# Linear attention beside a SwiGLU block: the order of x loads, statistics and normalisation around sixteen projection tiles

## The chip, the cores and the metric

The kernel runs on one core of a Trainium2 chip. The metric is the device time of one execution in microseconds (us). Five engines work side by side, each through its own list of instructions in order: TensorE (PE), ScalarE (ACT), VectorE (DVE), GpSimd (POOL) and SyncE (SP). SP and ACT also issue DMAs, each on a queue of its own.

## The reference

The input is x (2048 x 512), with bf16 weights. Both branches read the same layer-normalised rows.

```python
xn = _layernorm(x)                        # mean and variance over 512
q, k, v = split(xn @ wqkv)                # 32 heads of 16
pq, pk = phi(q), phi(k)                   # phi(t) = where(t > 0, t + 1, exp(t)) + 1e-6
kv = einsum("bhsd,bhse->bhde", pk, v);  z = sum over s of pk
o  = (pq @ kv) / (pq . z + 1e-6)
g  = silu(xn @ w_gate);  u = xn @ w_up    # F = 1792
out = x + o @ wo + (g * u) @ w_down
```

## The kernel before

The 2048 rows are cut into 16 tiles of 128 (`NT`). Row p*16 + t of x is partition p of tile t, so one DMA can load several neighbouring tiles for all partitions. The program writes down, tile by tile, what each engine does. `_Prog` turns this into one list per engine, in the order of writing, and adds a semaphore wait wherever an operation reads or overwrites what another engine or a DMA has written. Nothing is reordered afterwards: the order of the text is the order of the work on each engine.

First stage, per tile t:

- `xload` (L197) brings x; `wqkv_load` (L204) brings quarters of the q and k weights (128 rows each).
- DVE computes the statistics: `bns(t)` (bn_stats, L289) and `agg(t)` (bn_aggr, L292). `rstd_pow(t)` then adds epsilon (L310; on DVE for the tiles in `VD`, on POOL for the others) and POOL raises to the power -0.5 (L317). `stat(t)` is the three in a row.
- `xn_dve(t)` (L297) normalises into `xn_sb`. `xn(t)` does that and, from tile 3 on, issues a DMA transpose on SP (`transpose_dma`, L380) into `xnT`, which PE needs as the stationary operand. Tiles 0 to 2 are transposed on PE, by hand-written steps with filler matmuls in between.
- PE computes `kproj(t)` and `qproj(t)` (L389; the first parts at L402), four matmuls each. ACT takes the exponentials (L425, L431) and copies q (L435). `feat_k(t)` on DVE clips (L442) and adds max(k, 0) (L451) to give pk; POOL adds up z from pk (`zsum`, L507), two tiles behind.
- `gtacc(t)` (L515) accumulates xn transposed times pk in four PSUM banks. The product with the v weights is taken only once, after all tiles.

The start is written out by hand to tile 3. From tile 4 a loop runs, and two tables, `STAT` and `XN`, say after the features of which tile a later tile's statistics and normalisation are placed:

```python
STAT = {4: (8,), 5: (9,), 6: (10,), 7: (11, 12), 8: (13,), 9: (14, 15)}
XN = {4: (7,), 5: (8,), 6: (9,), 7: (10,), 8: (11, 12), 9: (13,), 10: (14, 15)}
```

In iteration 10, behind the transposes of tiles 14 and 15, SP issues tile 0's transpose (wanted only by the second stage), then the first halves of the gate and up weights (`whalf`, L219), the v weights, the output weights and the second half of the gate weights.

The second stage is the feed-forward: for each of four chunks of 512 rows and 14 column blocks, PE computes gate and up (L648), ACT the silu (L663) and DVE the product (L669). The attention output's matrices (L746, L769), the normalisation of pq by its denominator (L778 to L811) and the output tiles (L820, L831, L844) are woven in between. The first feed-forward matmuls need `xnT` of tiles 0 to 3 and the first weight halves.

Of the kernel before, what the change touches and what calls it, by code (L numbers as in the profile page):

```python
# [108 lines left out]
def bass_parallel_sum__linear_attn_block__swiglu_ffn__prompt_kernel(  # L109
# [13 lines left out]
    pe, act, dve, pool, sp = nc.tensor, nc.scalar, nc.vector, nc.gpsimd, nc.sync  # L123
    bf, f32 = dt.bfloat16, dt.float32

    with contextlib.ExitStack() as es:
        E = es.enter_context

        def sb(name, shape, d=bf):
            return E(nc.sbuf_tensor(name, [P] + shape, d))  # L130
# [6 lines left out]
        xnT = sb("xnT", [NDC, S])  # L137
# [50 lines left out]
        def bk(i):  # L188
            return ("bank", i)
# [5 lines left out]
        def xload(eng, h, t0, n, after=()):  # L195
            K.dma(
                eng, lambda: h.dma_start(x_sb[:, t0:t0 + n, :], xv[:, t0:t0 + n, :]),  # L197
                r=list(after), w=[("x", t0 + i) for i in range(n)],
            )

        def wqkv_load(eng, h, name, i, c0, n, after=()):
            K.dma(
                eng,
                lambda: h.dma_start(  # L204
                    wqkv_sb[:, c0:c0 + n, i * D:(i + 1) * D],
                    A_wqkv[c0 * P:(c0 + n) * P, i * D:(i + 1) * D].rearrange("(c p) f -> p c f", p=P),
                ),
                r=list(after), w=[(name, c0)],
            )
# [6 lines left out]
        def whalf(name, dst, src, h):  # L216
# [19 lines left out]
            r=[("ident",)], w=[("ident",)],  # L236
# [6 lines left out]
        wqkv_load("sp", sp, "wk", 1, 2, 2)  # L243
        xload("act", act, 2, 1)
        wqkv_load("act", act, "wq", 0, 0, 2)
        wqkv_load("sp", sp, "wq", 0, 2, 2)
        xload("act", act, 3, 1)
        xload("sp", sp, 4, 1)
        xload("act", act, 5, 1)
        xload("sp", sp, 6, 4, [("wq", 0), ("wq", 2)])  # L250
        xload("sp", sp, 10, 2)
        xload("sp", sp, 12, 4)

        cw = nc.const_aps.tensor(1.0, (P, P), bf)
        cx = nc.const_aps.tensor(1.0, (P, 512), bf)
# [32 lines left out]
        def bns(t):  # L288
            K.op("dve", lambda: dve.bn_stats(stats[:, t, :], x_sb[:, t, :]), r=[("x", t)], w=[("st", t)])  # L289

        def agg(t):
            K.op("dve", lambda: dve.bn_aggr(mv[:, t, :], stats[:, t, :]), r=[("st", t)], w=[("mv", t)])  # L292
# [8 lines left out]
                r=[("x", t), ("mv", t), ("rstd", t)], w=[("xn", t)],  # L301
            )

        VD = (1, 2, 3, 4)

        def rstd_pow(t):
            eng, h = ("dve", dve) if t in VD else ("pool", pool)
            K.op(
                eng,
                lambda: h.tensor_scalar(  # L310
                    out=vpe[:, t:t + 1], in0=mv[:, t, 1:2], scalar1=1e-5, scalar2=None, op0=ALU.add,
                ),
                r=[("mv", t)], w=[("vpe", t)],
            )
            K.op(
                "pool",
                lambda: pool.tensor_tensor(out=rstd[:, t:t + 1], in0=vpe[:, t:t + 1], in1=nhalf[:, :], op=ALU.pow),  # L317
                r=[("vpe", t), ("nhalf",)], w=[("rstd", t)],
            )

        def transpose_pe(t, b):
            tb = banks[b].bitcast(bf)[:, 0:512].rearrange("p (c s) -> p c s", c=NDC)
            K.op(
                "pe",
                [
                    (lambda c=c: pe.transpose(tb[:, c, :], xn_sb[:, t, c * P:(c + 1) * P], ident[:, :]))
                    for c in range(NDC)
                ],
                r=[("xn", t), ("ident",)], w=[bk(b)],
            )  # L330
            K.op(
                "act",
                lambda: act.activation(xnT[:, :, t * P:(t + 1) * P], tb, ACT.Copy),
                r=[bk(b)], w=[("xnT", t)],
            )
# [41 lines left out]
        def transpose_dma(t):  # L377
            K.dma(
                "sp",
                lambda: sp.dma_start_transpose(out=xnT[:, :, t * P:(t + 1) * P], in_=xn_sb[:, t, :]),  # L380
                r=[("xn", t)], w=[("xnT", t)],
            )


        def proj(t, b, lo, wname):
            K.op(
                "pe",
                [
                    (lambda c=c: pe.matmul(  # L389
                        banks[b], xnT[:, c, t * P:(t + 1) * P], wqkv_sb[:, c, lo:lo + D],  # L390
                        start=(c == 0), stop=(c == NDC - 1),
                    ))
                    for c in range(NDC)
                ],
                r=[("xnT", t), (wname, 0), (wname, 2)], w=[bk(b)],
            )

        def proj_part(src, key, b, lo, wname, h):
            K.op(
                "pe",  # L400
                [
                    (lambda c=c: pe.matmul(  # L402
                        banks[b], src[:, c, :], wqkv_sb[:, c, lo:lo + D],
                        start=(c == 0), stop=(c == NDC - 1),
                    ))
                    for c in (2 * h, 2 * h + 1)
                ],
                r=[key, (wname, 2 * h)], w=[bk(b)],
            )

        def kb(t):
            return 2 * (t % 2)

        def qb(t):
            return 2 * (t % 2) + 1

        def kproj(t):
            proj(t, kb(t), D, "wk")

        def qproj(t):  # L420
            proj(t, qb(t), 0, "wq")
# [7 lines left out]
        def exp_q(t):  # L429
            K.op(  # L430
                "act", lambda: act.activation(eq[:, t, :], banks[qb(t)], ACT.Exp),  # L431
                r=[bk(qb(t))], w=[("eq", t)],
            )
            K.op(
                "act", lambda: act.activation(pkq[:, t, 1, :], banks[qb(t)], ACT.Copy),  # L435
                r=[bk(qb(t))], w=[("pq", t)],
            )

        def clip(e, res):
            K.op(  # L440
                "dve",
                lambda: dve.tensor_scalar(  # L442
                    out=e, in0=e, scalar1=1.0, scalar2=1e-6, op0=ALU.min, op1=ALU.add,
                ),
                r=[res], w=[res],
            )

        def maxadd(dst, src, e, r, w):
            K.op(
                "dve",  # L450
                lambda: dve.scalar_tensor_tensor(  # L451
                    out=dst, in0=src, scalar=0.0, in1=e, op0=ALU.max, op1=ALU.add,
                ),
                r=r, w=w,
            )
# [25 lines left out]
        def first_feat():  # L481
            K.op(
                "dve",
                lambda: dve.tensor_tensor(out=pkq[:, 0, 0, :], in0=kpos[:, :], in1=ek[:, 0, :], op=ALU.add),
                r=[("kpos",), ("ek", 0)], w=[("pk", 0)],
            )

        def feat_k(t):
            e = t % NE
            clip(ek[:, e, :], ("ek", e))  # L490
            if t >= 2:
                zsum(t - 2, e)
            maxadd(pkq[:, t, 0, :], banks[kb(t)], ek[:, e, :], [bk(kb(t)), ("ek", e)], [("pk", t)])
# [30 lines left out]
        def stat(t):  # L524
            bns(t)
            agg(t)
            rstd_pow(t)

        def xn(t):
            xn_dve(t)  # L530
            if t >= 3:
                transpose_dma(t)

        bns(0)
        agg(0)
# [33 lines left out]
        agg(3)  # L569
        rstd_pow(3)  # L570
        first_feat()
        transpose_pe(2, 4)
        exp_k(1)
        first_eq()
        first_pq()
        qproj(1)
        kproj(2)
        xn(3)
        bns(4)
        agg(4)  # L580
        rstd_pow(4)
        feat_k(1)
        bns(5)
        xn(4)
        agg(5)
        rstd_pow(5)
        exp_q(1)
        exp_k(2)
        gtacc(0)
# [1 line left out]
        exp_q(2)  # L591
        gtacc(1)
        feat_k(2)
        stat(6)
        xn(5)
        kproj(3)
        exp_k(3)
        qproj(3)
        exp_q(3)
        feat_k(3)  # L600
        stat(7)
        xn(6)
        gtacc(2)

        STAT = {4: (8,), 5: (9,), 6: (10,), 7: (11, 12), 8: (13,), 9: (14, 15)}
        XN = {4: (7,), 5: (8,), 6: (9,), 7: (10,), 8: (11, 12), 9: (13,), 10: (14, 15)}

        for t in range(4, NT):
            kproj(t)
            exp_k(t)  # L610
            qproj(t)
            exp_q(t)
            feat_k(t)
            for i in STAT.get(t, ()):
                stat(i)
            for i in XN.get(t, ()):
                xn(i)
            if t == 10:
                transpose_dma(0)
                whalf("wg", wg_sb, B_w_gate, 0)  # L620
                whalf("wu", wu_sb, B_w_up, 0)
                wqkv_load("sp", sp, "wv", 2, 0, 4)
                wload("sp", sp, "wo", wo_sb, A_wo)
                whalf("wg", wg_sb, B_w_gate, 1)
            if t == 12:
                masks()
            if t >= 12:
                gtacc(t - 2)
            elif t < 11:
                gtacc(t - 1)  # L630
# [242 lines left out]
        for j in range(NJ):  # L873
# [11 lines left out]
            if NORM0 <= j < NORM0 + 3 * NT:  # L885
                i, ph = (j - NORM0) // 3, (j - NORM0) % 3
# [41 lines left out]
```

## Time and profile before

| | us |
|---|---|
| median of 3 runs | 214.53 |
| lowest, highest | 214.12, 214.85 |
| profiled execution | 215.17 |
| its span, first to last instruction | 213.9 |
| PE busy | 208.8 (98%) |
| DVE busy | 119.8 (56%) |
| POOL busy | 72.5 (34%) |
| ACT busy | 68.2 (32%) |
| mean granted clock of PE | 1.000 |

The profile shows one execution. Its span runs from the first to the last instruction; the device time includes what lies around it. Busy time counts computing instructions alone, not an engine's waits or the issue of DMAs. Matmuls overlap their neighbours and their ends are modelled, so the busy share of PE is a reading of how closely matmuls follow each other. Idle time of an engine matters only where the chain of waits passes through it. Times within the span are counted from its start: the projection stage lasts to 51.0 us, the second stage from there to the end.

### The profile page before, as it was taken

What the parts mean: (1) busy time and instruction counts of PE and PEld (TensorE: products, weight loads), DVE (VectorE), ACT (ScalarE), POOL (GpSimd) and SP (SyncE); (2) the same over time, 40 slices, a digit from 0 to 9 for tenths busy, and PEclk for the clock granted to TensorE, in tenths of its full rate; (3) what the DMA queues carried; (4) which work ended last, traced back from release to release, by engine and by line L of the source; (5) the groups of instructions that cost most, each with busy time, mean ns of one, the idle gap of its engine ahead of it and who ended that gap; (6) DMA issues with size and microseconds to landing.
All of it is one profiled execution on the core that took longest, in us unless ns stands there. A gap on an engine that the chain in (4) does not pass through costs nothing.

```text
span 213.9 us, 2779 instructions
## 1 busy us (share of the span) xinstructions
PE 208.8 (98%) x1001; PEld 96.7 (45%) x1001; DVE 119.8 (56%) x245; ACT 68.2 (32%) x119; POOL 72.5 (34%) x92
## 2 busy tenths in 40 slices
PE   8979989999999999999999999999999999999996
PEld 3434434444544444444444444444444444444454
DVE  4796888634454777355463765463656436374121
ACT  3476665666453332112031313122132213121000
POOL 3346777758104244042221441221404141222100
PEclk9999999999999999999999999999999999999999
DMA  5682233389994011102101011101011010110101
GB/s 184 242 211 49 49 31 72 77 272 365 225 368 124 0 25 25 49 3 49 25 26 49 0 28 49 29 20 49 3 49 25 25 25 28 27 48 26 49 28 51
DMA packets 28319, 16.45 MB, mean 77 GB/s; under 512 B 19088, under 2 KB 27920, under 8 KB 28304
## 3 DMA queue, kind: packets, MB, share of 16 engines
q1 hardware_dynamic: 27328, 15.34, 27.7%
q10 hardware_dynamic: 976, 0.92, 1.3%
q8 instruction: 8, 0.13, 0.3%
q14 instruction: 7, 0.06, 0.1%
HBM read 9.70 MB, written 2.10 MB: 55 GB/s over the span
## 4 chain that ended last, share of the span: by engine, by line
PE 89%; DMA 4%; DVE 4%; ACT 1%; issue 0%; POOL 0%; ACTq 0%
PE psum L648 45%; PE psum L831 23%; PE psum L389 7%; PE psum L820 6%; DMA xnT<-xn_sb 4%; PE psum L515 4%; PE psum L261 2%; DVE stats L289 1%; DVE pkq L451 1%; ACT ek L425 1%; DVE ek L442 1%; PE psum L402 0%; POOL rstd L317 0%; PE psum L746 0%; PE psum L769 0%
## 5 line engine op out<-in xcount | busy, mean ns | idle before, releaser
L663 ACT ACTIVATE sg<-psum 128x512 bf16<-128x512 f32 x56 | 33.4, 598 | 106.8 <-PE psum L648 106.0
L648 PE MATMUL psum<-xnT,wu_sb 128*128 128x512 bf16 x224 | 57.5, 379 | 0.0
L648 PE MATMUL psum<-xnT,wg_sb 128*128 128x512 bf16 x224 | 57.5, 379 | 0.0
L778 POOL TENSOR_TENSOR prod<-pkq,zb 128x512 f32<-128x512 bf16 x16 | 18.6, 1160 | 57.8 <-DVE pkq L451 57.8
L648 PEld LDWEIGHTS psum<-xnT,wu_sb 128*128 128x128 bf16 x224 | 21.9, 98 | 26.4 <-issue 0.2
L648 PEld LDWEIGHTS psum<-xnT,wg_sb 128*128 128x128 bf16 x224 | 21.9, 98 | 26.2
L844 DVE TENSOR_TENSOR out_sb<-psum,x_sb 128x512 bf16<-128x512 f32 (+1 forms) x17 | 11.2, 660 | 36.1 <-PE psum L831 36.1
L669 DVE TENSOR_TENSOR pkq<-psum,sg 128x512 bf16<-128x512 f32 x28 | 19.2, 687 | 18.6 <-PE psum L648 14.1
L802 POOL TENSOR_TENSOR pqn<-pkq,rden 128x512 bf16<-128x512 bf16 x16 | 16.9, 1055 | 36.6 <-DVE rden L796 36.6
L389 PE MATMUL psum<-wqkv_sb,xnT 128*128 128x512 bf16 x116 | 27.3, 379 | 1.9 <-DMA xnT<-xn_sb 1.9
L669 DVE TENSOR_TENSOR xn_sb<-psum,sg 128x512 bf16<-128x512 f32 x28 | 18.8, 671 | 14.2 <-PE psum L648 13.6
L831 PE MATMUL psum<-wd_sb,xn_sb 128*128 128x512 bf16 (+1 forms) x126 | 25.7, 355 | 0.0
L831 PE MATMUL psum<-wd_sb,pkq 128*128 128x512 bf16 x112 | 25.5, 379 | 0.0
L507 POOL TENSOR_TENSOR zacc<-zacc,pkq 128x512 f32<-128x512 f32 x15 | 17.3, 1155 | 6.4 <-DVE ek L442 6.0
L389 PEld LDWEIGHTS psum<-wqkv_sb,xnT 128*128 128x128 bf16 x116 | 11.1, 98 | 16.0 <-DMA xnT<-xn_sb 1.7
L831 PEld LDWEIGHTS psum<-wd_sb,xn_sb 128*128 128x128 bf16 x126 | 12.3, 98 | 11.9
L831 PEld LDWEIGHTS psum<-wd_sb,pkq 128*128 128x128 bf16 x112 | 11.0, 98 | 13.2
L820 PE MATMUL psum<-m_sb,eq 128*128 128x512 bf16 (+1 forms) x68 | 16.6, 366 | 0.0
L515 PE MATMUL psum<-pkq,xn_sb 128*128 128x512 bf16 x64 | 16.1, 379 | 0.0
L786 DVE TENSOR_REDUCE den<-prod 128x32 f32<-128x512 f32 x16 | 10.9, 684 | 5.7 <-POOL prod L778 5.7
L289 DVE BATCH_NORM_STATS2 stats<-x_sb 128x6 f32<-128x512 bf16 x16 | 10.9, 682 | 3.0 <-DMA x_sb<-in_A_x_dram 3.0
L425 ACT ACTIVATE ek<-psum 128x512 bf16<-128x512 f32 x15 | 9.0, 600 | 10.4 <-DVE mv L292 2.8
(67 smaller groups left out, 135.6 us busy)
## 6 DMA issues: line engine op xcount, KB each, us to landing
out_dram<-out_sb SPq DMA_DIRECT2D x15, 128.0 KB, 1.7
wg_sb<-in_B_w_gate_dram SPq DMA_DIRECT2D x2, 896.0 KB, 8.3
wu_sb<-in_B_w_up_dram SPq DMA_DIRECT2D x2, 896.0 KB, 6.7
wd_sb<-in_B_w_down_dram SPq DMA_DIRECT2D x1, 1792.0 KB, 9.7
x_sb<-in_A_x_dram SPq DMA_DIRECT2D x2, 512.0 KB, 4.4
wqkv_sb<-in_A_wqkv_dram ACTq DMA_DIRECT2D x2, 256.0 KB, 4.1
wqkv_sb<-in_A_wqkv_dram SPq DMA_DIRECT2D x2, 256.0 KB, 5.5
wqkv_sb<-in_A_wqkv_dram SPq DMA_DIRECT2D x1, 512.0 KB, 9.2
```

Of the source, the lines that this page charges most:

```text
L289: K.op("dve", lambda: dve.bn_stats(stats[:, t, :], x_sb[:, t, :]), r=[("x", t)], w=[("st", t)])
L389: (lambda c=c: pe.matmul(banks[b], xnT[:, c, t * P:(t + 1) * P], wqkv_sb[:, c, lo:lo + D], start=(c == 0), stop=(c == NDC - 1),))
L507: lambda: pool.tensor_tensor(out=zacc[:, :], in0=zacc[:, :], in1=pk, op=ALU.add),
L515: (lambda c=c: pe.matmul(banks[4 + c], xn_sb[:, t, c * P:(c + 1) * P], pkq[:, t, 0, :], start=(t == 0), stop=(t == NT - 1),))
L648: (lambda c=c: pe.matmul(banks[b], w_sb[:, c, fc * P:(fc + 1) * P], xnT[:, c, C * 512:(C + 1) * 512], start=(c == 0), stop=(c == NDC - 1),))
L663: lambda: act.activation(sg[:, j % NSG, :], banks[gb], ACT.Silu),
L669: lambda: dve.tensor_tensor(out=hT(C, fc), in0=banks[ub], in1=sg[:, j % NSG, :], op=ALU.mult,),
L778: lambda: pool.tensor_tensor(out=p, in0=pkq[:, t, 1, :], in1=zb[:, :], op=ALU.mult),
L802: lambda: pool.tensor_tensor(out=pqn[:, t % NPN, :].rearrange("p (h e) -> p h e", e=DH), in0=pkq[:, t, 1, :].rearrange("p (h e) -> p h e", ...
L820: (lambda g=g: pe.matmul(dst, pqnT(t)[:, g, :], m_sb[:, g, lo:hi], start=(g == 0), stop=False,))
L831: (lambda fc=fc: pe.matmul(dst, hT(C, fc)[:, jj * P:(jj + 1) * P], wd_sb[:, fc, lo:hi], start=False, stop=(fc == NFC - 1),))
L844: lambda: dve.tensor_tensor(out=o, in0=src, in1=x_sb[:, t, lo:hi], op=ALU.add),
```

## The change

The x loads of tiles 8 to 15 are no longer issued in a row on SP at the start. They go two tiles at a time, each behind one DMA transpose on SP: tiles 8 and 9 behind tile 3's, 10 and 11 behind tile 5's, 12 and 13 behind tile 6's, 14 and 15 behind tile 7's. Of the initial loads, tiles 6 and 7 remain as one.

The second half of the q weights is split into quarters: the third goes on SP's queue, the fourth on ACT's, ahead of x tile 3. Readers of the q weights wait for both, and so does the load of tiles 6 and 7.

Statistics are placed about a tile earlier. In the start, `bns(4)` stands ahead of `xn(3)`. In the loop, `STAT` places tile t+5 behind the features of tile t, and `XN0` places normalisations in front of the features, where `XN` had them behind. `VD` loses tile 4, whose epsilon is then added on POOL. Tile 0's DMA transpose moves from iteration 10 to iteration 7.

```diff
--- before
+++ after
@@ -243,13 +243,12 @@
         wqkv_load("sp", sp, "wk", 1, 2, 2)
         xload("act", act, 2, 1)
         wqkv_load("act", act, "wq", 0, 0, 2)
-        wqkv_load("sp", sp, "wq", 0, 2, 2)
+        wqkv_load("sp", sp, "wq", 0, 2, 1)
+        wqkv_load("act", act, "wq", 0, 3, 1)
         xload("act", act, 3, 1)
         xload("sp", sp, 4, 1)
         xload("act", act, 5, 1)
-        xload("sp", sp, 6, 4, [("wq", 0), ("wq", 2)])
-        xload("sp", sp, 10, 2)
-        xload("sp", sp, 12, 4)
+        xload("sp", sp, 6, 2, [("wq", 0), ("wq", 2), ("wq", 3)])
 
         cw = nc.const_aps.tensor(1.0, (P, P), bf)
         cx = nc.const_aps.tensor(1.0, (P, 512), bf)
@@ -301,7 +300,7 @@
                 r=[("x", t), ("mv", t), ("rstd", t)], w=[("xn", t)],
             )
 
-        VD = (1, 2, 3, 4)
+        VD = (1, 2, 3)
 
         def rstd_pow(t):
             eng, h = ("dve", dve) if t in VD else ("pool", pool)
@@ -392,7 +391,7 @@
                     ))
                     for c in range(NDC)
                 ],
-                r=[("xnT", t), (wname, 0), (wname, 2)], w=[bk(b)],
+                r=[("xnT", t), (wname, 0), (wname, 2)] + ([(wname, 3)] if wname == "wq" else []), w=[bk(b)],
             )
 
         def proj_part(src, key, b, lo, wname, h):
@@ -405,7 +404,7 @@
                     ))
                     for c in (2 * h, 2 * h + 1)
                 ],
-                r=[key, (wname, 2 * h)], w=[bk(b)],
+                r=[key, (wname, 2 * h)] + ([(wname, 3)] if wname == "wq" and h else []), w=[bk(b)],
             )
 
         def kb(t):
@@ -530,6 +529,10 @@
             xn_dve(t)
             if t >= 3:
                 transpose_dma(t)
+            if t == 3:
+                xload("sp", sp, 8, 2)
+            elif 5 <= t < 8:
+                xload("sp", sp, 2 * t, 2)
 
         bns(0)
         agg(0)
@@ -569,21 +572,22 @@
         agg(3)
         rstd_pow(3)
         first_feat()
+        bns(4)
+        xn(3)
+        agg(4)
+        rstd_pow(4)
         transpose_pe(2, 4)
         exp_k(1)
         first_eq()
         first_pq()
         qproj(1)
         kproj(2)
-        xn(3)
-        bns(4)
-        agg(4)
-        rstd_pow(4)
         feat_k(1)
         bns(5)
-        xn(4)
         agg(5)
         rstd_pow(5)
+        xn(4)
+        stat(6)
         exp_q(1)
         exp_k(2)
         gtacc(0)
@@ -591,32 +595,36 @@
         exp_q(2)
         gtacc(1)
         feat_k(2)
-        stat(6)
         xn(5)
+        stat(7)
         kproj(3)
         exp_k(3)
         qproj(3)
         exp_q(3)
+        xn(6)
         feat_k(3)
-        stat(7)
-        xn(6)
+        stat(8)
         gtacc(2)
 
-        STAT = {4: (8,), 5: (9,), 6: (10,), 7: (11, 12), 8: (13,), 9: (14, 15)}
-        XN = {4: (7,), 5: (8,), 6: (9,), 7: (10,), 8: (11, 12), 9: (13,), 10: (14, 15)}
+        STAT = {4: (9,), 5: (10,), 6: (11,), 7: (12, 13), 8: (14,), 9: (15,)}
+        XN0 = {4: (7,), 5: (8,), 6: (9,), 7: (10,), 8: (11,), 9: (12, 13), 10: (14, 15)}
+        XN = {}
 
         for t in range(4, NT):
             kproj(t)
             exp_k(t)
             qproj(t)
             exp_q(t)
+            for i in XN0.get(t, ()):
+                xn(i)
             feat_k(t)
             for i in STAT.get(t, ()):
                 stat(i)
             for i in XN.get(t, ()):
                 xn(i)
+            if t == 7:
+                transpose_dma(0)
             if t == 10:
-                transpose_dma(0)
                 whalf("wg", wg_sb, B_w_gate, 0)
                 whalf("wu", wu_sb, B_w_up, 0)
                 wqkv_load("sp", sp, "wv", 2, 0, 4)
```

## The prediction

> **What bounds the kernel now.** I first read busy time by engine and the chain of work that ended last: TensorE (PE) is busy 208.8 of 213.9 us, at full granted clock in all 40 slices, and carries 89% of the chain. So only a wait on PE's path can be worth time. The waits of PE, longest first, are three besides the start:
>
> ```profile
> PE psum L389 <- DMA xnT<-xn_sb: 1.9, 2, 1.2
> PE psum L261 <- PEq L913: 0.8, 1, 0.8
> PE psum L402 <- DMA wqkv_sb<-in_A_wqkv_dram: 0.3, 1, 0.3
> ```
>
> The timeline of PE places them. Columns are start, time, engine, line, operands; the bracket is the idle time before and what ended it:
>
> ```profile
> 7.50 0.59 PE L402 MATMUL psum<-wqkv_sb,xcT 128*128 128x512 bf16 x2
> 8.37 0.60 PE L402 MATMUL psum<-wqkv_sb,xcT 128*128 128x512 bf16 x2 [0.27 <-DMA wqkv_sb<-in_A_wqkv_dram]
> ...
> 13.35 1.03 PE L515 MATMUL psum<-pkq,xn_sb 128*128 128x512 bf16 x4
> 15.59 1.90 PE L389 MATMUL psum<-wqkv_sb,xnT 128*128 128x512 bf16 x8 [1.22 <-DMA xnT<-xn_sb]
> ...
> 30.28 1.03 PE L515 MATMUL psum<-pkq,xn_sb 128*128 128x512 bf16 x4
> 32.03 1.89 PE L389 MATMUL psum<-wqkv_sb,xnT 128*128 128x512 bf16 x8 [0.73 <-DMA xnT<-xn_sb]
> ```
>
> The bracket undercounts. A group of four that is followed without a wait hands over after 0.86 us (at 11.62, next at 12.49), though its modelled end is 1.03 after its start. PE could have gone on at 13.35 + 0.86 = 14.21 and at 30.28 + 0.86 = 31.14, so the two pauses cost 1.38 and 0.89 us: **2.27 us** on the path. In front of 8.37 the same reading gives 0.43.
>
> Why the data were late stands in the chain of waits and in the DMAs' issues and landings:
>
> ```profile
> 11.00 4.55 DMA xnT<-xn_sb
> 15.54 0.05 issue
> 15.59 1.90 PE psum L389 x8
> ...
> 27.28 4.62 DMA xnT<-xn_sb
> 31.90 0.14 issue
> ```
>
> Both are DMA transposes (L380), of tile 3 and of tile 9. The median of the 14 is 2.4 us from issue to landing; these two took 4.55 and 4.62. In front of tile 3's, on the same SP queue, went the x loads of tiles 6 to 9, 10 to 11 and 12 to 15, issued at 8.40, 8.79 and 9.26; the last landed at 14.90, the transpose 0.64 later. Tile 9's met no load. In its stretch (27 to 32 us) the DMA view shows two instruction fetches:
>
> ```profile
> q14 instruction: 1, 0.01, 1.8%
> q8 instruction: 1, 0.02, 1.8%
> ```
>
> In a usual 2.4 it would have landed at 29.7, 1.4 before PE's need at 31.14. So one transpose waits behind traffic, the other had too little lead.
>
> **The change part by part.**
>
> *x loads behind the transposes.* This takes 768 KB out of the way of tile 3's transpose (only tiles 6 and 7, 256 KB, stay ahead). Its normalisation waits today until 10.56 for rstd (0.44 of idle). In that hole now goes tile 4's bn_stats: the row L289 gives 0.61 us to the next start, so from 10.03 (the first features' start at 9.43, its 0.68 less an overlap of 0.08) to 10.64. The normalisation starts 0.08 later and the transpose at about 11.08. Its landing is bounded by 2.4 (median) and 4.55 (the row with 768 KB ahead). I take 2.5: the first x load, twice this size, landed 3.18 after its issue, at 11.58, while a transpose's own packets come in its second half. It lands at 13.6 against a need at 14.21, and the 1.38 goes. At the bad end, 15.63, 1.42 us remain.
>
> *What is late next.* Tile 4: PE wants it at 14.21 + 2.59 (the spacing of tiles in the PE rows) = 16.80. DVE's order is now clip and max-add of tile 1 (11.22 to 12.2, after ek at 11.18), bn_stats 5, aggregate, normalisation 4, ending near 13.35. The x load of tiles 8 and 9 is issued ahead of its transpose, at 12.4. By the 2.4 row it lands at 15.8, by 4.55 at 17.9. I take 16.1 (behind a 256 KB load that lands near 15.4): no wait. Tiles 5 to 8 follow the same sum and land 1 to 3 us ahead.
>
> *Statistics and normalisation a tile ahead.* In the loop, normalisation of tile t+3 stands before the features of tile t. Tile 9's comes near 23.0, its transpose at 23.3, landing 25.7 against a need at 14.21 + 6 x 2.59 = 29.75. A fetch that adds 2.2 (4.62 less 2.41) is covered, whichever transpose it hits: the 0.89 goes. DVE does the same work: 2.13 us of a tile's 2.59 (19.95 to 22.08), and its cyclic order stays clip, max-add, statistics, normalisation.
>
> *x data for DVE.* bn_stats of tile 8 comes near 17.3, its load is issued at 12.4; with the longest landing of any x load, 6.2, it is there at 18.6. A late one delays normalisation 7 (near 18.1) by 1.3, and its transpose still lands near 22.3, against 24.6. Later pairs have more. SP's queue gains three 0.45 us issues between transposes of 1.2: it stays under the 2.59 per tile.
>
> *VD without tile 4.* The add of epsilon goes from DVE (0.15) to POOL (0.22 to 0.39) ahead of a pow of 0.6; rstd is there at 12.1, the normalisation starts at 12.97: nothing.
>
> *Transpose of tile 0 and the weights.* SP issues the gate and up weights after the last transposes, today at 42.74 and 43.38. The up half lands at 51.64 and its first matmul starts at 51.89: 0.25 us of cover for a path that moves forward by 2.27. In the new order normalisations 14 and 15 stand before the features of tile 10. Normalisation 15 waits for its rstd until 34.45; the transposes issue at 33.7 and 34.9, tile 0's is no longer between, and the weights go out near 36.1. With 8.3 to landing, the up half is there by 45, before its need at 49.6. That hides; without it all but 0.25 us would be given back.
>
> *wq in two quarters, the second on ACT's queue.* The last of wq landed at 8.32, x tile 3 (the last of 768 KB on ACT's queue) at 8.14. Shifting 128 KB, wq should be complete near 8.14 (gain up to 0.18). x tile 3 lands later, by 0.1 to at most 0.81 (by 8.95 all ten loads had landed). It feeds bn_stats 3 at 8.24, then normalisation 2, which ends at 9.24 against PE's transpose at 9.68: 0.4 of cover, so at worst +0.3. Bounds -0.2 to +0.3; I take 0.
> The Trainium skill (DMA: Bandwidth & Descriptors, Queues, rings and completion order) says each DMA engine takes turns between the queues it has work for. That gives the same lateness of x tile 3, and the trace agrees: 896 KB on each queue, last landings 8.95 and 8.78.
>
> **Sum.** Profiled execution: 215.17 us, span 213.9 and 1.27 around it. Less 1.38 and 0.89 it is 212.9. The median of the three runs is 0.64 lower than that execution, 214.53; the same subtraction gives 212.3. All after the projections is PE work back to back and moves as one block.
>
> **Rivals.**
>
> *The SP queue still stretches the transposes.* Loads are now woven between them, and both would take 4.55. Tile 3's lands at 15.63, 1.42 is lost; tile 4's, 17.93, is then in time (18.22). Gain 2.27 - 1.42 = 0.85: 213.7. For it: the 4.55 row. Against: 256 KB ahead, not 768. A like case (213.4 to 213.6) is that the fetch's pause of 0.89 belongs to the profiled execution alone: the three times spread by 0.73.
>
> *The weights take the place of the wait.* If they went out no earlier, PE would stop at the first up matmul: gain 0.25, 214.3, no change. Against: the order written out above, 5 us of slack.
>
> *The change doesn't do what it says:* normalisation in front of the features is held up by POOL, and it comes out slower. The timeline shows it once:
>
> ```profile
> 37.55 1.64 DVE L297 TENSOR_SCALAR xn_sb<-x_sb,mv,rstd 128x512 bf16<-128x512 bf16 x2
> 37.56 1.16 POOL L507 TENSOR_TENSOR zacc<-zacc,pkq 128x512 f32<-128x512 f32 x1
> ```
>
> The first of the two took 1.32 where the row's least is 0.38: 0.93 more while POOL summed z. If each of the nine normalisations 7 to 15 met that, DVE would lose 8.4 us; its idle time before the clip (0.46 a tile, seven tiles) returns 3.2. The lag of 5.2 meets 1.7 us of slack (the sum over pk starts 4.33 after its tile's key projection, 2.59 + 1.73; pk is done at 2.6). PE loses 3.4, net +1.2: 215.7. It decides from 0.8 us more per normalisation. Against: z's sum starts at the clip and lasts 1.16, while max-add and statistics take 1.3 before the next normalisation, as in the old loop.
> A rule of the Trainium skill (SBUF — State Buffer, Who interferes with whom) speaks for this rival: a VectorE tensor_scalar in a two-port mode and a GpSimd instruction lock each other out for the whole instruction. The trace agrees at 37.55. By the rule with POOL's whole 1.16 for each, the same sum gives 9 x 1.16 - 3.2 - 1.7 = 5.5, net +3.3: 217.8.
>
> **How the numbers follow.** Forecast (both pauses gone) 0.68, stretched transposes or a fetch only in the profile 0.12, weights 0.07, lock-out 0.08, something not named 0.05, split evenly. A change of 0.3% (0.64 us) is about what these runs can tell from none. Faster: 0.68 + 0.12 + 0.02 = 0.82; same 0.07 and a little, 0.08; slower 0.10. The range takes the forecast with the early stage's bounds, 0.2 below and 0.3 above, and the runs' spread, and reaches over the first rival: 211.8 to 213.9.
>
> **What would show it.** After the change PE's waits should hold no line of L389 on a DMA; tile 3's transpose issued near 11.1 and landing before 14.2; tile 9's near 23.3; the weights out near 36; the feed-forward's first matmul near 48.75 rather than 51.02; normalisations near 0.4 us. Wrong would be: a wait at tile 3 or 4 with an x load in flight (first rival), one on the up weights (second), normalisations over 1.2 us with PE waiting on DVE (third), or a hold-up before 14 us from x tile 3 worth over 0.3.

## The result, and the profile after

The changed kernel takes 212.82 us (median of 6 runs, 212.67 to 213.16), the kernel before 214.54 beside it: a ratio of 0.9921, 95% interval 0.9906 to 0.9937. That is faster by 1.7 us (1.35 to 2.0), where 2.2 were forecast. The profiled execution took 213.16 us with a span of 211.88, 2.05 less than the span before.

The waits of PE in the changed kernel (lines of the code have moved: the projections are now L388 and L401, the feed-forward L656):

```profile
PE psum L401 <- DMA wqkv_sb<-in_A_wqkv_dram: 0.9, 2, 0.6
PE psum L260 <- PEq L921: 0.8, 1, 0.8
PE psum L388 <- DMA xnT<-xn_sb: 0.2, 1, 0.2
PE psum L363 <- DVE xc_sb L341: 0.2, 1, 0.2
```

Of the 1.9 us that L389 waited for DMA transposes, 0.2 is left. The 0.9 at L401, against 0.3 at L402 before, lies ahead of 8.2 us, where the first weights land. Even so PE is ready for tile 3 at 14.10, against 14.21 before. In a second profile of the changed kernel no such wait stands. The timeline of PE shows tile 3 following without a bracket, and where the rest sits:

```profile
13.24 1.03 PE L514 MATMUL psum<-pkq,xn_sb 128*128 128x512 bf16 x4
14.10 1.89 PE L388 MATMUL psum<-wqkv_sb,xnT 128*128 128x512 bf16 x8
...
21.01 1.03 PE L514 MATMUL psum<-pkq,xn_sb 128*128 128x512 bf16 x4
22.20 1.89 PE L388 MATMUL psum<-wqkv_sb,xnT 128*128 128x512 bf16 x8 [0.16 <-DMA xnT<-xn_sb]
...
48.96 1.03 PE L656 MATMUL psum<-xnT,wg_sb 128*128 128x512 bf16 x4
```

Read as before (a group hands over after 0.86), the pause at tile 6 costs 21.01 + 0.86 = 21.87 to 22.20, 0.33 us. The feed-forward starts at 48.96 instead of 51.02. From there to the end it is 162.9 us in both profiles, so the whole difference of the two spans arises in the projection stage. The chain of waits names tile 6's transpose, and the DMA view from 17 to 23 us holds one instruction fetch, a single packet of 1.56 us from 19.23:

```profile
17.34 4.73 DMA xnT<-xn_sb
22.06 0.14 issue
22.20 1.89 PE psum L388 x8
```

```profile
q8 instruction: 1, 0.02, 1.6%
```

### The profile page after: what moved, and what is told of

It reads as the page before. It is cut to its first block, busy times and chain, and to the rows that moved or that the text cites. A ratio compares the mean times of both kernels' runs of the same rounds, so it can differ in the third digit from the quotient of the medians.

```text
span 211.9 us, 2784 instructions
## 1 busy us (share of the span) xinstructions
PE 207.7 (98%) x1001; PEld 95.9 (45%) x1001; DVE 118.9 (56%) x244; ACT 68.1 (32%) x119; POOL 73.1 (35%) x93
## 4 chain that ended last, share of the span: by engine, by line
PE 89%; DMA 5%; DVE 4%; ACTq 1%; issue 0%; ACT 0%
PE psum L656 46%; PE psum L839 23%; PE psum L388 8%; PE psum L828 7%; PE psum L514 4%; DMA x_sb<-in_A_x_dram 3%; DMA xnT<-xn_sb 2%; DVE stats L288 1%; DVE pkq L450 1%; DVE xn_sb L296 1%; PE psum L754 0%; PE psum L777 0%; ACTq L204 0%; DVE ek L441 0%; DVE pkq L483 0%
## 5 line engine op out<-in xcount | busy, mean ns | idle before, releaser
L656 PE MATMUL psum<-xnT,wg_sb 128*128 128x512 bf16 x224 | 57.5, 379 | 0.0
L656 PE MATMUL psum<-xnT,wu_sb 128*128 128x512 bf16 x224 | 57.5, 379 | 0.0
L656 PEld LDWEIGHTS psum<-xnT,wu_sb 128*128 128x128 bf16 x224 | 21.9, 98 | 26.4
L656 PEld LDWEIGHTS psum<-xnT,wg_sb 128*128 128x128 bf16 x224 | 21.9, 98 | 26.2
L388 PE MATMUL psum<-wqkv_sb,xnT 128*128 128x512 bf16 x116 | 27.3, 379 | 0.2 <-DMA xnT<-xn_sb 0.2
L388 PEld LDWEIGHTS psum<-wqkv_sb,xnT 128*128 128x128 bf16 x116 | 11.1, 98 | 13.9 <-ACT eq L430 0.6
```

Source lines behind the costliest of these rows:

```text
L388: (lambda c=c: pe.matmul(banks[b], xnT[:, c, t * P:(t + 1) * P], wqkv_sb[:, c, lo:lo + D], start=(c == 0), stop=(c == NDC - 1),))
L656: (lambda c=c: pe.matmul(banks[b], w_sb[:, c, fc * P:(fc + 1) * P], xnT[:, c, C * 512:(C + 1) * 512], start=(c == 0), stop=(c == NDC - 1),))
```

## The experiments

In every profile the time at which PE could have begun tile 3 (end of the second sum over pk), the pauses behind it and the start of the feed-forward add up, to within 0.05: start = ready + 34.53 + pauses. (A wait for the up weights comes behind that start and is not in the sum.) The 34.53 is that of an execution without a pause (48.42 - 13.89). For the first profile of the kernel before it gives 14.21 + 34.53 + 1.38 + 0.89 = 51.01, where 51.02 was measured. All times in us; the medians are of all runs, the last two columns of the one profiled:

| kernel | median | ratio, 95% interval | ready | pauses after that, by the profile |
|---|---|---|---|---|
| before | 214.54 | | 14.21 | 1.38 tile 3, 0.89 tile 9 |
| before, again | 214.51 | 0.9996 (0.9974 to 1.0018) | 13.65 | 1.74 tile 3, 0.11 tile 8, 0.44 up weights |
| changed | 212.82 | 0.9921 (0.9906 to 0.9937) | 14.10 | 0.33 tile 6 |
| changed, again | 212.66 | 0.9925 (0.9901 to 0.9948) | 13.89 | none |
| loads only | 213.44 | 0.9947 (0.9930 to 0.9965) | 13.86 | 0.34 tile 7, 0.39 up weights |
| loads, tile 0 early | 213.38 | 0.9950 (0.9930 to 0.9969) | 14.28 | 0.95 tile 9 |
| order only | 214.06 | 0.9981 (0.9966 to 0.9996) | 14.12 | 1.60 tile 3 |
| late weights | 214.56 | 0.9995 (0.9979 to 1.0010) | 14.34 | 0.92 tile 6, 1.23 up weights |
| q weights in one | 212.64 | 0.9912 (0.9894 to 0.9930) | 14.09 | 0.78 tile 6 |
| the same, again | 212.96 | 0.9932 (0.9911 to 0.9954) | 13.71 | 0.42 tile 8 |
| later pairs | 212.88 | 0.9930 (0.9907 to 0.9953) | 13.92 | none |
| later, q in one | 212.64 | 0.9920 (0.9899 to 0.9942) | 13.85 | none |
| the same, again | 212.65 | 0.9921 (0.9900 to 0.9942) | 14.24 | none |
| xn behind features | 213.79 | 0.9970 (0.9954 to 0.9986) | 14.05 | 0.18 tile 8, 0.79 tile 9 |

**Loads only.** From the kernel before:

```diff
-        xload("sp", sp, 6, 4, [("wq", 0), ("wq", 2)])
-        xload("sp", sp, 10, 2)
-        xload("sp", sp, 12, 4)
+        xload("sp", sp, 6, 2, [("wq", 0), ("wq", 2)])
...
             if t >= 3:
                 transpose_dma(t)
+            if t == 3:
+                xload("sp", sp, 8, 2)
+            elif 5 <= t < 8:
+                xload("sp", sp, 2 * t, 2)
```

> The kernel before with the x loads of tiles 8 to 15 moved behind the transposes of tiles 3, 5, 6 and 7; the order of statistics and normalisation, tile 0's transpose and the q weights stay as before. Theory A (two separate causes, two separate cures: the loads cure tile 3's transpose, the order cures the lead of the later ones): tile 3's transpose lands near 13.5 and the pause of 1.38 us at 14.2 is gone; a pause of up to 0.9 us stays where an instruction fetch meets a transpose, since the lead of a transpose is still 1.4 us. Time near 213.2, between 213.1 and 213.9. Theory B (loads woven between transposes stretch them, and only the longer lead pays for that): new pauses at tiles 4 and 6 to 8, 0.5 us or more in sum, and a time of 213.7 to 214.5.

```profile
12.99 1.03 PE L513 MATMUL psum<-pkq,xn_sb 128*128 128x512 bf16 x4
13.86 1.89 PE L387 MATMUL psum<-wqkv_sb,xnT 128*128 128x512 bf16 x8
...
49.98 1.02 PE L650 MATMUL psum<-xnT,wu_sb 128*128 128x512 bf16 x4 [0.23 <-DMA wu_sb<-in_B_w_up_dram]
```

Tile 3's transpose landed at 13.53 and its pause is gone; the kernel gains 1.1 us. Tile 6's transpose, with an x pair in front and no fetch, took 2.8 us, not 4.55: the woven loads stretch little. Tile 7's took 4.06 with a fetch in it, and PE paused 0.34. Theory B, which wanted 0.5 us or more of new pauses and at least 213.7, falls. Next late are the up weights, landing at 49.84: a cause that theory A had not counted in this kernel. The time lies within theory A's range, 0.2 above the value it named.

**Order only.** The changed kernel with the loads of x and the q weights of the kernel before:

```diff
-        wqkv_load("sp", sp, "wq", 0, 2, 1)
-        wqkv_load("act", act, "wq", 0, 3, 1)
+        wqkv_load("sp", sp, "wq", 0, 2, 2)
...
-        xload("sp", sp, 6, 2, [("wq", 0), ("wq", 2), ("wq", 3)])
+        xload("sp", sp, 6, 4, [("wq", 0), ("wq", 2)])
+        xload("sp", sp, 10, 2)
+        xload("sp", sp, 12, 4)
...
-            if t == 3:
-                xload("sp", sp, 8, 2)
-            elif 5 <= t < 8:
-                xload("sp", sp, 2 * t, 2)
```

> The changed kernel with the x loads and the q weights issued as before (all at the start), so that the order of statistics, normalisation and tile 0's transpose alone is changed. Theory A: tile 3's transpose still waits behind 768 KB of x and lands near 15.6, the pause of about 1.4 us at tile 3 stays; no later pause, since the lead of a transpose covers a fetch. Time near 213.7 if the fetch's pause of 0.89 belongs to usual executions of the kernel before, near 214.5 if it belongs to its profiled execution alone. Theory B (the remaining 0.16 us of idle at tile 6 in the changed kernel is due to x loads in front of its transpose, not to the fetch): here no pause at tile 6 whatever the fetch does; Theory A lets one of up to 0.3 us stand there if the fetch falls on it again.

```profile
13.26 1.03 PE L515 MATMUL psum<-pkq,xn_sb 128*128 128x512 bf16 x4
15.72 1.90 PE L389 MATMUL psum<-wqkv_sb,xnT 128*128 128x512 bf16 x8 [1.44 <-DMA xnT<-xn_sb]
```

Tile 3's transpose, behind the x loads again, took 4.38 and landed at 15.68. Behind it PE never waits. The gain of 0.47 lies between the two numbers of theory A, and the run says why nothing waits at tile 6: without an x pair to issue first, its transpose goes out at 17.13 and lands at 19.68, as the fetch at 19.53 begins. So the fetch all but missed tile 6, and this run does not decide between the theories on its pause. Both halves together, 1.09 (interval 0.75 to 1.50) and 0.47 (0.09 to 0.73), make 1.56 of the changed kernel's 1.72: two cures that add up as far as these intervals tell, as theory A of the loads-only kernel has it.

**Late weights.** From the changed kernel:

```diff
             if t == 10:
+                pass
+            if t == 13:
+                K.join("sp", [("pk", 13)])
                 whalf("wg", wg_sb, B_w_gate, 0)
                 whalf("wu", wu_sb, B_w_up, 0)
```

> The changed kernel with the gate, up, v and output weights held back until pk of tile 13 is ready, near 42.3 us, which is when the kernel before issued them. It tests whether the change needs the earlier weights. Theory A (the weights had 0.25 us of cover before, so a path that moves forward by 2.06 needs them earlier): the up half, issued near 43.0, lands 7.2 to 8.3 later, near 50.2 to 51.2; PE waits for it from 49.8 on, 0.4 to 1.4 us; time 213.2 to 214.2. Rival (the weights are off the path either way): no wait of PE on a weight, 212.8.

The weights went out at 43.17, the up half landed at 51.74, and the gain is gone. The timeline of PE:

```profile
49.79 1.03 PE L659 MATMUL psum<-xnT,wg_sb 128*128 128x512 bf16 x4
51.88 1.02 PE L659 MATMUL psum<-xnT,wu_sb 128*128 128x512 bf16 x4 [1.06 <-DMA wu_sb<-in_B_w_up_dram]
```

The time, 214.56, is 0.4 above the range of theory A: the up half went out at 43.60, 0.6 later than I reckoned, and the profiled execution had 0.92 at tile 6 besides. The rival (weights off the path) falls. What the profile puts down to the weights is 1.23 us (49.79 + 0.86 = 50.65 to 51.88); that tile 6 paused as long in the other executions is not shown.

**Loads, and tile 0's transpose earlier.** To the loads-only kernel:

```diff
-            if t == 10:
+            if t == 7:
                 transpose_dma(0)
+            if t == 10:
                 whalf("wg", wg_sb, B_w_gate, 0)
```

> The kernel before with the x loads behind the transposes of tiles 3, 5, 6 and 7, and tile 0's transpose moved from iteration 10 to iteration 7, so that the weights go out 1.3 us earlier; statistics and normalisation stay in their old order. Theory A (with the loads alone the first up weights are the next thing late, by 0.39 us; taking tile 0's transpose from in front of them clears it): the up half is issued near 40.2, lands near 48.5, no wait on it; time 213.0 to 213.1. Rival (with the loads alone the pauses at the transposes are what is left and the weights do not matter): 213.4 as with the loads alone.

The up half went out at 40.84, landed at 49.03, and PE did not wait for it. It would have been in time without the pause at tile 9 as well: the need would then have been at 49.7. So far the profile is theory A's. The time is the rival's, 213.38, the same as with the loads alone. In the profile a fetch at 27.07 and another at 28.00 hit tile 9's transpose (4.68 us) for 0.95, but that execution, at 214.11 us, was the slowest of the eight: its pause does not explain the median, which stays open. The weights' part of the gain is shown in the profile, not in the time.

**The kernel before, again.**

> The kernel before, unchanged, profiled a second time. Theory A (the pause at tile 9 is an instruction fetch that meets a transpose with 1.4 us of lead, and comes in every execution, at one transpose or another): a pause of PE of 0.5 to 0.9 us after 20 us, with a transpose that takes 4 us or more and a fetch within it. Rival (the fetch fell on a transpose in the first profiled execution alone): no pause after tile 3's, and a span near 213.0.

The waits of PE:

```profile
PE psum L389 <- DMA xnT<-xn_sb: 1.6, 1, 1.6
PE psum L261 <- PEq L913: 0.8, 1, 0.8
PE psum L648 <- ACT gt_sb L678: 0.3, 1, 0.3
```

```profile
50.05 1.03 PE L648 MATMUL psum<-xnT,wg_sb 128*128 128x512 bf16 x4
51.35 1.02 PE L648 MATMUL psum<-xnT,wu_sb 128*128 128x512 bf16 x4 [0.28 <-ACT gt_sb L678]
```

The fetch came at 25.45 and hit tile 8's transpose (3.84 us), whose lead covered all but 0.11 us. So the pause of 0.89 was not a fixed part of the kernel; both statements were partly wrong. The last line of the waits is put down to ACT, but it is the up weights. The up half landed at 51.21, and PE started 0.14 behind that, as behind the late landings of the other runs (49.84 and 49.98, 51.74 and 51.88). ACT's two copies ended at 50.84 and 51.33. In the first profile the same matmul started at 51.89, while the second copy still ran until 52.31, so it does not need that copy. With no pause at tile 9, the weights were late by 0.44.

**The q weights in one load.** From the changed kernel, twice:

```diff
-        wqkv_load("sp", sp, "wq", 0, 2, 1)
-        wqkv_load("act", act, "wq", 0, 3, 1)
+        wqkv_load("sp", sp, "wq", 0, 2, 2)
```

> The changed kernel with the second half of the q weights as one load on SP's queue again. Theory A: the split is worth what PE gained ahead of tile 3, 0.1 us (14.10 instead of 14.21): time 212.8 to 213.0. Rival (the split makes x tile 3 late by 0.32 us, which holds DVE up, so without it the kernel is faster): bn_stats of tile 3 starts at 8.25 instead of 8.49, tile 3's transpose is issued at 11.05 instead of 11.32, and the time is 212.5 to 212.7.

> The changed kernel with the second half of the q weights as one load again, a second comparison, beside the changed kernel on one chip. Theory A (the split is worth nothing either way): within 0.15 us of the changed kernel. Rival (the split costs 0.2 us by making x tile 3 late): 0.15 to 0.3 us less than the changed kernel.

Once 0.2 us below the changed kernel, once 0.3 above it, with intervals that overlap: the split moves nothing that these runs can tell. The ready times, 14.09 and 13.71, lie among those of the other kernels.

**Later pairs.** From the changed kernel; the second form has the q weights in one load as well:

```diff
-            elif 5 <= t < 8:
-                xload("sp", sp, 2 * t, 2)
+            elif 6 <= t < 9:
+                xload("sp", sp, 2 * t - 2, 2)
```

> The changed kernel with the x pairs 10-11, 12-13 and 14-15 each issued one transpose later, behind those of tiles 6, 7 and 8. In the changed kernel tile 6's transpose was ready at 16.6 us, waited for SP to issue the x pair, went out at 17.34, met an instruction fetch at 19.23 and landed at 22.06 against a need at 21.87. Theory A (the remaining pause is the fetch on a transpose that the x pair's issue had made late): here it goes out near 16.7, lands near 19.1, ahead of the fetch; tile 7's may meet the fetch but has over 1 us to spare; no pause of PE on a transpose, 0.3 us less than the changed kernel, 212.4 to 212.6. Rival (the pause moves on to the transposes of tiles 7 to 9, whose lead is no longer): a pause of 0.2 to 0.8 us there, 212.7 to 213.2.

> The same later x pairs, and the second half of the q weights as one load on SP's queue again. Theory A (the split is worth nothing either way): 212.3 to 212.6, the same as with the split. Rival (the split holds x tile 3 and with it DVE up by 0.2 us or more): 212.1 to 212.3.

> The later x pairs with the q weights' second half as one load, a second comparison, beside the changed kernel on one chip. Theory A (the later pairs take away a pause that only some executions have): 0.1 to 0.4 us less than the changed kernel, and no pause of PE on a transpose in the profile. Rival (nothing is left in the pauses): the same within 0.1 us.

Tile 6's transpose went out at 16.96, 16.46 and 17.28 and landed before 19.8; fetches met those of tiles 7, 8 or 9 (3.8 to 4.3 us), and none of the three profiles has a pause on a transpose. The medians, 212.88, 212.64 and 212.65, are not clearly below the changed kernel's 212.82 and 212.66. Theory A's gain of 0.3 us is missed with the split; the repeat, 0.01 below the changed kernel on the same chip, is its rival's. That three profiles have no pause on a transpose does not prove the pause gone: the changed kernel itself has none in one of two. No version here beats the changed kernel by more than can be told.

**The changed kernel, again.**

> The changed kernel, unchanged, profiled a second time beside the others. Theory A (which transpose the instruction fetch meets differs between executions; in the changed kernel it costs 0 to 0.9 us): again a fetch between 19 and 26 us; if it meets tile 6's transpose a pause of 0.3 to 0.9 us after 21 us, otherwise none and a span near 211.4. Time 212.7 to 212.9. Rival (the fetch always meets tile 6's): the pause again, at 22 us.

The waits of PE, where no projection waits for a transpose:

```profile
PE psum L260 <- PEq L921: 0.8, 1, 0.8
PE psum L363 <- DVE xc_sb L341: 0.4, 1, 0.4
```

The fetch came at 24.03 and met tile 9's transpose (4.28 us, landed 27.59), which was needed at 29.43 and had 1.8 us to spare. So the rival (always tile 6) falls.

**Normalisation behind the features.** From the changed kernel, in `feat_k`, and without the calls in front of it:

```diff
-        def feat_k(t):
+        def feat_k(t, mid=()):
...
             maxadd(pkq[:, t, 0, :], banks[kb(t)], ek[:, e, :], [bk(kb(t)), ("ek", e)], [("pk", t)])
+            for i in mid:
+                xn(i)
```

> The changed kernel with the normalisations of tiles 7 to 15 directly behind the max-add of the features, where POOL's sum over pk of 1.16 us is under way, in place of in front of the clip. It prices the lock-out rival. Theory A (POOL's sum holds the normalisation up, but DVE has 0.46 us of idle a tile and the transposes 4 us of lead): the first normalisation of each tile takes about 0.9 instead of 0.4 us, DVE loses some 0.5 us a tile, and the time stays at 212.8 to 213.1. Rival (a DVE that is held up becomes the bound, as the prediction's slower case had it): PE waits for pk or for a transpose, 1 us or more, 213.8 to 216. If there is no hold-up at all, the normalisations stay at 0.4 us.

DVE's and POOL's timelines:

```profile
19.76 1.36 DVE L296 TENSOR_SCALAR xn_sb<-x_sb,mv,rstd 128x512 bf16<-128x512 bf16 x1
22.75 0.41 DVE L296 TENSOR_SCALAR xn_sb<-x_sb,mv,rstd 128x512 bf16<-128x512 bf16 x1
24.96 1.36 DVE L296 TENSOR_SCALAR xn_sb<-x_sb,mv,rstd 128x512 bf16<-128x512 bf16 x1
```

```profile
19.81 1.15 POOL L508 TENSOR_TENSOR zacc<-zacc,pkq 128x512 f32<-128x512 f32 x1
22.86 1.31 POOL L508 TENSOR_TENSOR zacc<-zacc,pkq 128x512 f32<-128x512 f32 x1
25.02 1.15 POOL L508 TENSOR_TENSOR zacc<-zacc,pkq 128x512 f32<-128x512 f32 x1
```

The hold-up is real: of the nine normalisations 7 to 15 four take 1.09 to 1.36 and five 0.40 to 0.41; where DVE is the quick one, as at 22.75, POOL's sum is the longer one (1.31). The Trainium skill (SBUF — State Buffer, Who interferes with whom) has a VectorE instruction in a two-port mode and a GpSimd instruction lock each other out for the whole instruction; 1.36 is 0.2 more than POOL's 1.15, so the trace agrees that DVE was held through POOL's sum. The time is 213.79, 1 us over the changed kernel. PE did not wait for pk: the transposes lost lead (tile 9's went out at 26.35 rather than 23.18), and a fetch on it then cost 0.79, after 0.18 at tile 8. Theory A was too low. The rival's price was reached at its lower end: PE waited 0.97 us in all for transposes, one of the two ways it named, but with a fetch in both.

## Why the prediction was right, and where it was off

- **Bound and readings.** Right: nothing changed after the projections, and both pauses were on the path.
- **Tile 3.** Forecast: issue 11.08, landing 13.6, pause gone. Profiled: 11.32 and 13.81, and 11.10 and 13.60 in the second execution; no pause. The loads-only kernel shows that the x loads did it. The prediction's 768 KB are tiles 10 to 15; eight tiles of 128 KB, 1024 KB, were moved, since tiles 8 and 9 had been part of the load that landed at 11.58.
- **Stretched transposes (first rival).** An x pair in front costs up to 1.0 us (tiles 4 and 6 to 8 without a fetch, in all kernels with woven loads: 2.4 to 3.4 for 2.4), not 2.1. Ruled out as a price; it does eat lead. The rows say where the price comes from: without a fetch, a transpose whose load in front still had 2 us or more to go landed 0.5 to 0.8 us behind that load, in the kernel before (tile 3, 14.90 and 15.54) as behind the pairs (tile 4 of the changed kernel, 15.73 and 16.32).
- **Lead.** Tile 9's transpose at 23.18 (forecast 23.3). The failed step is "a fetch ... is covered, whichever transpose it hits". I worked it out for tile 9, with 4.0 us of lead, and let it stand for tiles 5 to 8, with 1 to 3 us. In the changed kernel and its variants the fetch came between 19 and 28 us, on tiles 6 to 9. Tile 6's transpose, issued at 17.34 behind an x pair's issue, had 2.1 us of slack and lost 2.3; the pause was 0.33 in one profile of the changed kernel and none in the other, and up to 0.92 in its variants. It took the x pair and the fetch together. With the pair and no fetch, tile 6's transpose took 2.8 to 3.3 in five profiles and PE did not wait; with both it took 4.7 to 4.9 in three, and PE waited in each. The prediction priced the two apart. Its 2.2 for a fetch came from a transpose that had met two.
- **Weights (second rival).** Forecast out at 36.1, profiled 36.80 and 36.26: no wait. The step "that hides; without it all but 0.25 would be given back" is borne out by the late weights: the median gave all back, and 1.23 us of that stands at the up weights in the profile. What I had missed is that the kernel before itself can run into this wait, as in its second profile, where the fetch did little harm.
- **Lock-out (slower rival).** Normalisations 7 to 15 took 0.38 to 0.50 in both profiles, as the cyclic order had let expect. Its mechanism is real at another place in the order, its price there 1 us.
- **q weights, x tile 3.** x tile 3 landed at 8.46, 0.32 later, within the bounds; PE was ready at 14.10 and 13.89 against 14.21 and 13.65. The 0 taken stands.
- **The sum.** For the profiled execution it gave 212.9, and 213.16 was measured: 0.33 at tile 6, less 0.1 of an earlier start. The step that failed is the transfer to the median: "the same subtraction gives 212.3". Profiled executions of the two kernels differ by 2.0 twice (215.17 and 213.16, 214.62 and 212.58), though the pauses of the kernel before lay elsewhere the second time (1.74 + 0.11 + 0.44 instead of 1.38 + 0.89). What is missing there is the 0.33 at tile 6 less 0.11 of start in the first pair; in the second it is the start, which came 0.24 later in the changed kernel. The medians differ by 1.7 (1.35 to 2.0), so the pauses of one profile, taken in full, were too much for the median by 0.5; about half of that stands in the profiles, and the rest lies within the interval and stays open. The range holds 212.82 in part because it was drawn up to 213.9 for the first rival, which did not come; that is room, not insight. How often a fetch falls on which transpose in a run without a profile was not measured.

## What to carry to other kernels

Here a small, urgent transfer landed only behind the large one issued ahead of it on its queue, 0.5 to 0.8 us later while that one was still under way: large loads belong behind it, as late as their reader allows. Before a pause is subtracted, ask what comes next just in time (here weights with 0.25 us of cover), and move that too. A pause from something that comes at another moment in each execution is part of one profile, not of the median: take a second profile before it goes into the sum, and give every tile the lead, not only the one that was hit.

## What the runs showed of the hardware

An instruction fetch of 16 KB, a single packet of 0.9 to 1.6 us, came between 19.2 and 28.2 us in all 14 profiles, at another time in two executions of one kernel (28.06 and 25.45; 19.23 and 24.03). In 13 of them a transpose in flight then took 3.8 to 5.9 us instead of 2.4. The second stage says the same of its own transposes of 128x512. In the 14 profiles, 28 of them met a 16 KB fetch and took 3.2 to 4.4 us (3.9 to 4.4 where no other transfer was under way); the 229 that met no fetch took 2.4 to 2.6, though 106 of these ran beside other transfers. The other 23 met a fetch of 8 KB alone. Still, the 28 stand at two places of the program, and no run moved a fetch: that it is the cause rests on coincidence, if on a close one.

The start varies too: PE was ready for tile 3 between 13.65 and 14.34 us. In the kernel before, most of that was swallowed by the wait for tile 3's transpose (ready at 14.21 and 13.65, tile 3 begun at 15.59 and 15.39); in the changed one it goes through to the end (14.10 and 13.89, feed-forward at 48.96 and, without a pause, 48.42).
